# The last of 32 attention groups in two quarters of the tokens, one behind the other

## The chip, the cores and the metric

The kernel runs on one core of one Trainium2 chip. A core has five engines that work side by side and wait for one another by semaphores: PE (TensorE, matrix products; PEld is its loading of weights), DVE (VectorE), ACT (ScalarE), POOL (GpSimd) and SP, which here only issues DMA transfers. Products land in PSUM, which has eight banks of 128 partitions x 512 numbers; a tile of 128 x 512 fills one. The metric is device time in microseconds (us) of one execution, median of several runs.

## The reference

The result is a gated sum of two branches over an input x of 2048 tokens x 512 channels:

- branch A is attention with 32 heads of 16 channels: `softmax(q k^T / 4) v` for each head, all heads side by side, times `wo` (512 x 512);
- branch B is a layer norm followed by a two-layer MLP across the tokens (2048 to 1792 to 2048) with a gelu between;
- `out = g * A + (1 - g) * B` with `g = sigmoid(sum(x * gate_w))` for each token.

All inputs and the output are float32.

## The kernel before, in words

To keep float32 accuracy most operands are split into a high and a low part, and a product is three matrix products: hi x hi, hi x lo, lo x hi. `split` (lines 63 to 66) makes the parts: a copy and a subtraction.

After the projections and the MLP's first layer (lines 165 to 397), which the change leaves alone, comes the long part, lines 399 to 810. The attention runs in `NG` = 32 **groups**: 16 pairs of heads, for each of two halves of the tokens (1024 query tokens a half). A group has 64 units of scores: 16 chunks of 128 keys, two heads, two quarters of 512 query tokens (`qb`). For a unit, `score` (line 689) multiplies 64 rows of stacked parts of k and q into a PSUM bank; the two heads of a pair lie on rows 0 to 63 and 64 to 127, so that PE computes a score of each side by side. Two units share a tile `s`, and one ACT instruction takes the exponential of both (line 709) into `pt`. `apply_v` (line 657) multiplies `pt` by the head's v (16 columns and a column of ones, which gives the sum of the exponentials) and adds into the one bank `av`, four blocks of 32 partitions.

The group's loop (lines 712 to 757) goes in 11 **phases** (`ph`), ten of six units and one of four; two phases are a **two** (`two`), five of them in a group. The order in a phase is written out by hand: scores, then deferred work, then `apply_v` for the units of the phase before (`late`). Between the scores stand **dense** products of other work: the MLP's second layer (`second_layer`), and the attention's output product (`project`), 128 rows of the result at a time. A dense step is cut in halves of 64 rows: the upper half runs in a two's first phase and the lower half in its second, each beside a score on the other half of PE's rows. `put` and `put_outputs` lay the steps out over the twos (`dense[two]`, four to six each), and `call` hangs other work on a two (`calls`). A small POOL instruction (`token`) keeps the two halves apart, and all dense work adds into the single bank `dn`.

When a group ends, `evacuate` (line 629) copies `av` to `ot` on DVE, stores the rows to DRAM (`o_d`), and puts `invert` (maximum and reciprocal of the sums, whole tile) into `slow`, a list from which one item is taken in each second phase; its result is stored (`r_d`) by the list `stores`. When four groups of a half are done, `fetch_o` (line 511) loads their rows and the reciprocals, the latter spread over 16 rows for each head, and puts `divide` (product, then split) into `slow`; the parts are `o_parts[half, k]`, k = 0 to 3. For the second half of the tokens k = 3 holds only three pairs of heads (96 rows), since the fourth pair is the last group itself. `EARLY` = 9 is the number of products (of 12) for k = 0 to 2; for tiles 8 to 15 `project` adds those into `base` rows held on chip. In the last group tiles 12 to 15 of these are still being done.

After the last group (lines 764 to 808) eight banks `pa` take, for each of the eight tiles of 128 tokens in the second half, the three products for k = 3 (`others`) and those of the last pair, whose o is not fetched but taken from `ot`: a product with `sums_of` spreads the sums over the rows, DVE takes maximum, reciprocal, product and split (in two halves m of 256 columns of each head and quarter), and 16-row products with `wq`, the last 32 rows of `wo`, finish the banks. Each bank is then scaled by the gate and added to its row, five by DVE (line 805), three by ACT and POOL (lines 801, 802), and sent out, 256 KB a row block, on the queues of SP and ACT.

At the end all engines load a flag and jump over a general version of the attention that these inputs do not need (lines 813 to 866).

## Time and profile before

| what | value |
|---|---|
| median of 3 runs | 1336.42 us |
| lowest and highest of the runs | 1335.47 and 1336.7 us |
| the profiled execution's own time | 1335.31 us |
| its span, first to last instruction | 1333.4 us |
| busy: PE, ACT, DVE, POOL | 99%, 82%, 31%, 15% |
| mean granted clock of PE | 0.996 |
| first score of the last group | at 1278.98 us |
| copy of the last group's sums | at 1311.52 us |

The profile is of one execution. A row of the timeline gives start, length, engine, line, operation, result and operands, shapes, count, and in brackets the idle time before it with what ended it. The chain of work is followed back from the last instruction to what released each step. An engine's name with a q is its queue of instructions, as in SPq for DMA issues. A product's row lasts longer than the interval at which products follow on each other, since they are pipelined; the chain shows the intervals.

### The profile page before, as it was taken

The numbers are of one execution on the slowest core, as the hardware profiler recorded it, in microseconds if no ns is written. First come the engines' busy times: TensorE is split into PE (matmuls) and PEld (weight loads), VectorE is DVE, ScalarE is ACT, GpSimd is POOL, SyncE is SP. The second block draws the span as 40 slices with busy tenths as digits, with TensorE's granted clock in tenths as the row PEclk, the third lists the DMA queues.
The fourth block names the chain that finished last, engine by engine and source line by source line (L and its number), as shares of the span: only waits on it lengthen the run. The fifth ranks groups of instructions, "written<-read, shape, count | busy, mean of one in ns | idle before, by whom it ended". The sixth has DMA issues, their size and how long they took to land.

```text
span 1333.4 us, 32411 instructions
## 1 busy us (share of the span) xinstructions
PE 1314.6 (99%) x13288; PEld 770.0 (58%) x13288; DVE 413.5 (31%) x625; ACT 1096.3 (82%) x1264; POOL 202.3 (15%) x468
## 2 busy tenths in 40 slices
PE   9999999999999999999999999999999999999996
PEld 6888778876555555555555555455554555545553
DVE  3596571454121111222322111222111222132324
ACT  3344343447999999999999999999999999999993
POOL 0210254443011011011000011000110110100001
PEclk9999999999999999999999999999999999999998
DMA  3587643327343333334555344545333334454511
GB/s 119 165 275 294 206 119 95 95 75 156 73 85 65 61 73 83 67 75 96 121 109 129 68 76 90 100 111 125 61 65 73 77 68 81 72 113 108 108 53 67
DMA packets 93240, 138.41 MB, mean 104 GB/s; under 512 B 14149, under 2 KB 53211, under 8 KB 90011
## 3 DMA queue, kind: packets, MB, share of 16 engines
q1 hardware_dynamic: 92650, 135.46, 42.7%
q8 instruction: 107, 1.75, 0.6%
q10 hardware_dynamic: 432, 0.79, 0.2%
q14 instruction: 51, 0.41, 0.1%
HBM read 99.63 MB, written 36.56 MB: 102 GB/s over the span
## 4 chain that ended last, share of the span: by engine, by line
PE 94%; ACT 2%; DMA 1%; DVE 1%; SPq 0%; issue 0%; POOL 0%; POOLq 0%; DVEq 0%; ACTq 0%
PE av L665 35%; PE s L700 26%; PE acc L357 12%; PE dn L738 11%; PE acc L73 10%; ACT pt L709 2%; DMA o_sum<-r 1%; PE dn L685 1%; PE acc L184 0%; DMA wv_raw<-in_A_wqkv_dram 0%; DVE sums L783 0%; SPq L419 0%; POOL w_lo L66 0%; DVE base L805 0%; DVE lo L66 0%
## 5 line engine op out<-in xcount | busy, mean ns | idle before, releaser
L709 ACT ACTIVATE pt<-s 128x1024 f32<-128x1024 f32 x1024 | 964.9, 1028 | 33.9 <-PE s L700 26.6
L700 PE MATMUL s<-qs,ks 64*128 64x512 f32 x2048 | 527.4, 421 | 3.0 <-ACT pt L709 3.0
L665 PE MATMUL av<-pt,v 128*17 128x256 f32 x8192 | 510.6, 381 | 0.0
L700 PEld LDWEIGHTS s<-qs,ks 64*128 64x128 f32 x2048 | 301.0, 184 | 207.8 <-ACT pt L709 155.4
L665 PEld LDWEIGHTS av<-pt,v 128*17 128x17 f32 x8192 | 205.2, 97 | 259.6 <-issue 125.3
L738 PE MATMUL dn<-u_hi,w_hi 64*128 64x512 f32 x428 | 182.3, 426 | 0.7 <-POOL token L742 0.7
L66 POOL TENSOR_TENSOR w_lo<-w_raw,w_hi 128x512 fp32r<-128x512 f32 (+1 forms) x128 | 154.4, 1209 | 136.5 <-ACT w_hi L65 111.4
L738 PE MATMUL dn<-u_lo,w_hi 64*128 64x512 f32 x428 | 169.6, 396 | 0.0
L738 PE MATMUL dn<-u_hi,w_lo 64*128 64x512 f32 x428 | 168.4, 393 | 0.0
L742 POOL MEMSET token<- 1x1 f32 x320 | 29.3, 92 | 875.8 <-PE dn L738 552.2
L631 DVE COPY ot<-av 128x512 f32<-128x512 f32 x32 | 22.1, 692 | 352.9 <-PE av L665 347.5
L644 DVE RECIPROCAL rt<-rt 128x512 f32<-128x512 f32 x31 | 103.9, 3353 | 1.1
L65 ACT CAST w_hi<-w_raw 128x512 fp32r<-128x512 f32 (+1 forms) x67 | 37.8, 566 | 65.9 <-PE acc L357 59.9
L357 PE MATMUL acc<-h_hi,w_lo 128*128 128x512 f32 x224 | 89.2, 398 | 0.3 <-POOL w_lo L66 0.3
L357 PE MATMUL acc<-h_hi,w_hi 128*128 128x512 f32 x224 | 89.0, 397 | 0.0
L357 PE MATMUL acc<-h_lo,w_hi 128*128 128x512 f32 x224 | 88.8, 396 | 0.0
L738 PEld LDWEIGHTS dn<-u_lo,w_hi 64*128 64x128 f32 x428 | 79.2, 185 | 3.4
L738 PEld LDWEIGHTS dn<-u_hi,w_lo 64*128 64x128 f32 x428 | 79.0, 185 | 3.6
L738 PEld LDWEIGHTS dn<-u_hi,w_hi 64*128 64x128 f32 x428 | 78.7, 184 | 3.7 <-POOL token L742 1.0
L65 DVE CAST w_hi<-w_raw 128x512 fp32r<-128x512 f32 (+1 forms) x61 | 22.4, 378 | 124.4 <-PE dn L738 66.8
L434 DVE TENSOR_SCALAR row<-dn,b2x,omg 128x512 f32<-128x512 f32 x16 | 13.0, 810 | 147.8 <-PE dn L738 106.5
L73 PE MATMUL acc<-xt_hi,wc_hi 128*128 128x512 f32 x128 | 49.8, 389 | 0.0
(131 smaller groups left out, 1065.8 us busy)
## 6 DMA issues: line engine op xcount, KB each, us to landing
w_raw<-in_B_w_dram SPq DMA_DIRECT2D x96, 256.0 KB
ks<-kp SPq DMA_DIRECT2D x192, 128.0 KB
qs<-qp SPq DMA_DIRECT2D x256, 64.0 KB
qp<-pc SPq DMA_DIRECT2D x16, 768.0 KB
x<-in_A_x_dram SPq DMA_DIRECT2D x32, 256.0 KB
kp<-pc SPq DMA_DIRECT2D x16, 512.0 KB
w_raw<-in_B_w_dram SPq DMA_DIRECT2D x32, 128.0 KB
bp<-row SPq DMA_DIRECT2D x16, 256.0 KB
```

The lines of the kernel that those rows point to most:

```text
L65: copy(hi, src)
L66: sub(lo, src, hi.bitcast(F32), ALU.subtract)
L73: nc.tensor.matmul(ps, a, b, start=start and n == 0, stop=stop and n == last)
L357: nc.tensor.matmul(p, a, b, start=first and k == 0, stop=last and k == 2)
L631: nc.vector.tensor_copy(ot, av)
L644: nc.vector.reciprocal(rt, rt)
L665: nc.tensor.matmul(av[32 * j : 32 * j + VC, i * QC : (i + 1) * QC], v[:, c, g % NP * 2 + i, :], pt[:, h * QC : (h + 1) * QC], start=added[ ...
L685: nc.tensor.matmul(ps, a, b, start=start, stop=stop)
L700: nc.tensor.matmul(s[:, m, :], kt[grp][rows, c * P : (c + 1) * P], qt[grp][rows, qb * NB : (qb + 1) * NB], start=True, stop=True,)
L709: nc.scalar.activation(pt, s, AF.Exp, scale=SCALE)
L738: mm = nc.tensor.matmul(ps, a[half], b[half], start=first and not second, stop=last and bool(second))
L742: fence = nc.gpsimd.memset(token, 0.0)
```

## The change

**The last group in two quarters.** In the last group the order of units becomes all of the first quarter of its tokens (qb = 0), then all of the second. It has twelve phases of 6, 6, 6, 6, 4, 4 units for each quarter. `av` then holds one quarter in 256 columns, a block of 32 partitions for each of two heads and two halves of the quarter; `evacuate` copies 256 columns, once after each quarter.

**Dense products on all rows.** In the last group no dense half stands beside a score. The last four of the nine early products of tiles 13 to 15 (`full`) come in phases 0 to 5, two a phase, on all rows, after `apply_v`. In phases 6, 7, 9, 10 and 11 `rest_early` does the three products for k = 3 of tiles 8 to 12 and adds them to their rows; in phase 8 `divide_last` starts the division of the first quarter. Items of `slow` are taken in every phase of this group.

**The order before it.** Tiles 10 and 11 of the second layer take 8 twos instead of 9. The first products of tiles 13 to 15 are five each instead of four. Opening the end's memory, and the calls of `fetch_o`, come up to two twos earlier; the reciprocals of group 30 are stored, and the last fetch is called, at the start of the third phase of the last group.

**The end.** Tiles 0 to 3 of the eight (the first quarter) need only the last pair's products, tiles 5, 6 and 7 the three for k = 3 as well. The last pair's products use 64 rows (both heads, `wq` laid out so). The division is done once for each quarter. Tiles 0 and 2 and tile 7 go by ACT and POOL, the others by DVE; the add of tile 2 waits for the second quarter's split.

```diff
--- before.py
+++ after.py
@@ -63,7 +63,7 @@
     def split(hi, lo, src, copy, sub):
 
         copy(hi, src)
-        sub(lo, src, hi.bitcast(F32), ALU.subtract)
+        return sub(lo, src, hi.bitcast(F32), ALU.subtract)
 
     def products(ps, pairs, start=True, stop=True):
 
@@ -499,13 +499,12 @@
             sums_of.rearrange("p (j r) -> p j r", r=32),
             ident.rearrange("p (j r) -> p j r", r=32)[:, :, DH:VC].broadcast_to([P, P // 32, 32]),
         )
-        wq.extend(end.tile([P, 2, D], F32R, name=f"wq{n}") for n in range(2))
-        raw = end.tile([P, 2, D], F32, name="wq_raw")
+        wq.extend(end.tile([P, D], F32R, name=f"wq{n}") for n in range(2))
+        raw = end.tile([P, D], F32, name="wq_raw")
         nc.gpsimd.memset(raw, 0.0)
         for j in range(4):
-            nc.sync.dma_start(
-                raw[32 * j : 32 * j + DH], a_wo[(H - 2) * DH : H * DH, :].rearrange("(i r) c -> r i c", i=2)
-            )
+            r0 = (H - 2 + j % 2) * DH
+            nc.sync.dma_start(raw[32 * j : 32 * j + DH], a_wo[r0 : r0 + DH, :])
         slow.append((two + 5, lambda: split(wq[0], wq[1], raw, nc.vector.tensor_copy, nc.vector.tensor_tensor)))
 
     def fetch_o(half, k, pairs=4):
@@ -571,8 +570,11 @@
 
     TWOS = 5
-    dense, calls = {}, {}
+    LAST = [6, 6, 6, 6, 4, 4] * 2
+    dense, calls, full = {}, {}, {}
 
     def put(steps, at, sizes):
         for n in sizes:
@@ -599,7 +601,7 @@
     first, at = steps[:30], put(steps[30:], 0, [6] * 2)
     for t in range(NS):
         if t:
-            at = put(second_layer(t), at, [6, 6] + [4] * 6 + [6] if t > 9 else [6] * 4 + [4] * 3 + [6])
+            at = put(second_layer(t), at, [6, 6] + [4] * 6 + [6] if t > 11 else [6] * 4 + [4] * 3 + [6])
         if t == 7:
             call(at - 8, fetch_o, 0, 0)
             call(at - 5, fetch_o, 0, 1)
@@ -612,13 +614,23 @@
     call(at - 5, fetch_o, 1, 1)
     assert at - 5 > (NP + 8) * TWOS + 4
     call(at, open_end)
-    at = put_outputs(range(NS - 3, NS), 0, 4, at)
-    assert at == (NP + 12) * TWOS + 7
-    call(at - 2, fetch_o, 1, 2)
+    call(at + 1, fetch_o, 1, 2)
+    assert at > (NP + 12) * TWOS + 1
+    at = put_outputs(range(NS - 3, NS), 0, 5, at)
     at = put_outputs(range(NH, NS - 3), 0, EARLY, at, [5, 4])
-    at = put_outputs(range(NS - 3, NS), 4, EARLY, at)
-    assert at == NG * TWOS
-    call((NG - 1) * TWOS + 2, fetch_o, 1, 3, 3)
+    assert at == (NG - 1) * TWOS
+    for t in range(NS - 3, NS):
+        steps, load = project(t, 5, EARLY)
+        call(at - 1, load)
+        full[at, 0], full[at, 1] = steps[:2], steps[2:]
+        at += 1
+
+    def store():
+        while stores:
+            stores.pop()()
+
+    call((NG - 1) * TWOS + 1, store)
+    call((NG - 1) * TWOS + 1, fetch_o, 1, 3, 3)
 
     token = out_pool.tile([1, 1], F32, name="token", bufs=1)
     av = ps_av.tile([P, NB], F32, name="av")
@@ -628,9 +640,10 @@
 
     def evacuate(g):
         ot = out_pool.tile([P, NB], F32, name="ot")
+        if g == NG - 1:
+            nc.vector.tensor_copy(ot[:, :QC], av[:, :QC])
+            return ot[:, :QC]
         nc.vector.tensor_copy(ot, av)
-        if g == NG - 1:
-            return ot
         half, p = divmod(g, NP)
         k, p = divmod(p, 4)
         blocks = [(slice(32 * j, 32 * j + VC), slice(j * QC, (j + 1) * QC)) for j in range(4)]
@@ -656,18 +669,23 @@
 
     def apply_v(g, units, last):
 
-        for pair in zip(*([u for u in units if u[2] == qb] for qb in range(2))):
-            for i, c, qb, pt in pair:
-
-                added[qb] += 1
+        final = g == NG - 1
+        key = 0 if final else 2
+        for pair in zip(*([u for u in units if u[key] == n] for n in range(2))):
+            for unit in pair:
+                i, c, qb, pt = unit
+
+                n = unit[key]
+                added[n] += 1
                 for h in range(2):
-                    j = 2 * qb + h
+                    j = 2 * h + i if final else 2 * qb + h
+                    at = 0 if final else i * QC
                     nc.tensor.matmul(
-                        av[32 * j : 32 * j + VC, i * QC : (i + 1) * QC],
+                        av[32 * j : 32 * j + VC, at : at + QC],
                         v[:, c, g % NP * 2 + i, :],
                         pt[:, h * QC : (h + 1) * QC],
-                        start=added[qb] == 1,
-                        stop=added[qb] == 2 * NS,
+                        start=added[n] == 1,
+                        stop=added[n] == (1 if final else 2) * NS,
                     )
         if last:
             added[:] = 0, 0
@@ -689,7 +707,7 @@
         def score(grp, i, n, done):
 
             nonlocal open_s
-            c, qb = n // 2, (n + i) % 2
+            c, qb = (n % NS, n // NS) if grp == NG - 1 else (n // 2, (n + i) % 2)
             if open_s is None:
                 open_s = ps_s.tile([P, 2, NB], F32, name="s"), ptp.tile([P, 2, NB], F32, name="pt")
                 m = 0
@@ -709,23 +727,44 @@
                 nc.scalar.activation(pt, s, AF.Exp, scale=SCALE)
                 open_s = None
 
+        def rest(t, ps, stop=True):
+
+            for n, (a, b) in enumerate(o_matmuls(1, t, EARLY, 3 * ND)):
+                nc.tensor.matmul(ps, a, b, start=n == 0, stop=stop and n == 2)
+
+        def rest_early(t):
+            ps = ps_dn.tile([P, D], F32, name="dn")
+            rest(t, ps)
+            output(t, ps, rows[t])
+
+        def divide_last(qb, ot, totals):
+
+            nc.tensor.matmul(totals, sums_of, ot, start=True, stop=True)
+            sums, hi, lo = (
+                end.tile([P, QC], dt, name=f"{name}{qb}") for name, dt in (("sums", F32), ("hi", F32R), ("lo", F32R))
+            )
+            nc.vector.tensor_scalar_max(sums, totals, LEAST_SUM)
+            nc.vector.reciprocal(sums, sums)
+            nc.vector.tensor_mul(sums, ot, sums)
+            step = split(hi, lo, sums, nc.vector.tensor_copy, nc.vector.tensor_tensor)
+            return hi, lo, step
+
         for grp in range(NG):
             at = [0, 0]
-            for ph in range(2 * TWOS + 1):
+            final = grp == NG - 1
+            for ph, n_s in enumerate(LAST if final else [6] * 2 * TWOS + [4]):
                 if ph == 0 and grp + 1 < NG:
                     qt[grp + 1] = load_q(grp + 1)
                 if ph == 1 and grp + 1 < NG:
                     kt[grp + 1] = load_k(grp + 1)
                 two, second = divmod(ph, 2)
                 two += grp * TWOS
-                if ph == 2 * TWOS:
-                    n_s, beside = 4, []
-                elif second:
-                    n_s = 6
-                else:
+                if ph == 2 * TWOS and not final:
+                    beside = []
+                elif not second:
                     for what, *args in calls.get(two, ()):
                         what(*args)
-                    n_s, beside = 6, [step(*args) for step, *args in dense.get(two, ())]
+                    beside = [step(*args) for step, *args in dense.get(two, ())]
                 units = []
                 for n in range(n_s - len(beside)):
                     i = (n + second + 1) % 2
@@ -744,18 +783,30 @@
                     if done and second:
                         done()
                 if second:
-                    while stores:
-                        stores.pop()()
+                    store()
                     if len(ready) < 2:
                         split_weight(nc.vector.tensor_copy)
+                if second or final:
                     for n, (ready_at, step) in enumerate(slow):
                         if ready_at <= two:
                             slow.pop(n)[1]()
                             break
-                if late:
-                    apply_v(*late)
-                late = grp, units, ph == 2 * TWOS
+                ot = apply_v(*late) if late else None
+                late = grp, units, ph in (5, 11) if final else ph == 2 * TWOS
+                if final:
+                    for step, *args in full.get((two, second), ()):
+                        ps, a, b, first, last, done = step(*args)
+                        nc.tensor.matmul(ps, a, b, start=first, stop=last)
+                        if done:
+                            done()
+                    if ph == 6:
+                        last_ot = ot
+                    if ph == 8:
+                        parts = [divide_last(0, last_ot, ps_dn.tile([P, D], F32, name="dn")[:, :QC])]
+                    elif ph > 5:
+                        rest_early(NH + ph - 6 - (ph > 8))
         last_ot = apply_v(*late)
+        assert not slow and not stores
     psum_ctx.close()
 
     ptp_ctx.close()
@@ -765,47 +816,60 @@
         tc.tile_pool(name="ps_end", bufs=1, space=PSUM, reuse_waits="tile") as ps_end,
         tc.manual_schedule(engines=engines),
     ):
...
+        pa = {t: ps_end.tile([P, D], F32, name=f"pa{t}") for t in (5, 6, 0, 1, 2, 3, 4, 7)}
+
+        def last_pair(qb, m):
+
+            for n, (a, b) in enumerate(((0, 0), (0, 1), (1, 0))):
+                for h in range(2):
+                    t = 4 * qb + 2 * h + m
+                    at = slice(h * HALF, (h + 1) * HALF)
+                    lhs = parts[qb][a][at, m * P : (m + 1) * P]
+                    nc.tensor.matmul(pa[t], lhs, wq[b][at], start=t < 5 and n == 0, stop=n == 2)
+
+        def row_of(t):
+            return rows[NH + t], g[:, NH + t : NH + t + 1], of[(NH + t) * P : (NH + t + 1) * P, :]
+
+        def scaled(t):
+            res = end.tile([P, D], F32, name=f"res{t}")
+            nc.scalar.activation(res, pa[t], AF.Copy, scale=row_of(t)[1])
+            return res
+
+        def add(t, res):
+            row = row_of(t)[0]
+            return nc.gpsimd.tensor_tensor(row, res, row, ALU.add)
+
+        def finish(t):
+            row, gate, _ = row_of(t)
+            nc.vector.scalar_tensor_tensor(row, pa[t], gate, row, ALU.mult, ALU.add)
+
+        def put_row(t, queue):
+            row, _, dst = row_of(t)
+            queue.dma_start(dst, row)
+
+        last_pair(0, 0)
+        res0 = scaled(0)
+        add(0, res0)
+        put_row(0, nc.sync)
+        res2 = scaled(2)
+        parts.append(divide_last(1, last_ot, pa[4][:, :QC]))
+        last_pair(0, 1)
+        for t in (5, 6, 7):
+            rest(NH + t, pa[t], stop=False)
+
+        tc.add_manual_dep(add(2, res2).ins, parts[1][2].ins.name, SYNC, reason="one port")
+        put_row(2, nc.scalar)
+        for t in (1, 3):
+            finish(t)
+            put_row(t, nc.sync)
+        last_pair(1, 0)
+        last_pair(1, 1)
+        for t in (4, 6, 5):
+            finish(t)
+            put_row(t, nc.scalar if t == 6 else nc.sync)
+        res7 = scaled(7)
+        add(7, res7)
+        put_row(7, nc.scalar)
     end_ctx.close()
     att_ctx.close()
 
```

More of the change, by code (lines that the diff above doesn't have):

```diff
@@ L767, in gated_mix @@
     ):
-        pa = [ps_end.tile([P, D], F32, name=f"pa{t}") for t in range(8)]
-        def others(*tiles):
-            for t in tiles:
-                for n, (a, b) in enumerate(o_matmuls(1, NH + t, EARLY, 3 * ND)):
-                    nc.tensor.matmul(pa[t], a, b, start=n == 0, stop=False)
-        others(0)
-        nc.tensor.matmul(pa[7], sums_of, last_ot, start=True, stop=True)
-        tiles = [end.tile([P, NB], dt, name=name) for name, dt in (("sums", F32), ("hi", F32R), ("lo", F32R))]
@@ L778, in gated_mix @@
-        sums, hi, lo = ([x.rearrange("p (i m c) -> p m i c", i=2, m=2)[:, m] for m in range(2)] for x in tiles)
-        totals, last = (x.rearrange("p (i m c) -> p m i c", i=2, m=2) for x in (pa[7], last_ot))
-        for m in range(2):
-            nc.vector.tensor_scalar_max(sums[m], totals[:, m], LEAST_SUM)
-        for m in range(2):
-            nc.vector.reciprocal(sums[m], sums[m])
-            nc.vector.tensor_mul(sums[m], last[:, m], sums[m])
-            split(hi[m], lo[m], sums[m], nc.vector.tensor_copy, nc.vector.tensor_tensor)
@@ L786, in gated_mix @@
-        others(2, 4, 6, 1, 3)
-        behind = []
-        for m in range(2):
-            for i in range(2):
-                for n, (a, b) in enumerate(((hi, 0), (hi, 1), (lo, 0))):
-                    for j in range(4):
-                        at = slice(32 * j, 32 * j + DH)
-                        nc.tensor.matmul(pa[2 * j + m], a[m][at, i, :], wq[b][at, i, :], start=False, stop=i == 1 and n == 2)
-            if m == 0:
-                others(5, 7)
-            for j in range(4):
-                t = 2 * j + m
-                row, gate, dst = rows[NH + t], g[:, NH + t : NH + t + 1], of[(NH + t) * P : (NH + t + 1) * P, :]
-                if j == 1 or j == 3 and m == 0:
-                    res = end.tile([P, D], F32, name=f"res{t}")
-                    nc.scalar.activation(res, pa[t], AF.Copy, scale=gate)
-                    nc.gpsimd.tensor_tensor(row, res, row, ALU.add)
-                    behind.append((dst, row))
-                else:
-                    nc.vector.scalar_tensor_tensor(row, pa[t], gate, row, ALU.mult, ALU.add)
-                    nc.sync.dma_start(dst, row)
@@ L807, in gated_mix @@
-        for dst, row in behind:
-            nc.scalar.dma_start(dst, row)
+        pa = {t: ps_end.tile([P, D], F32, name=f"pa{t}") for t in (5, 6, 0, 1, 2, 3, 4, 7)}
[6 more added lines that the diff above has]
+                    nc.tensor.matmul(pa[t], lhs, wq[b][at], start=t < 5 and n == 0, stop=n == 2)
```

## The prediction

> **What bounds the kernel now.** I read the page first (busy shares, then the chain of work that ended last), then the table by stage, then that chain in order of time, then the timeline around the last group.
>
> ```profile
> PE 1314.6 (99%) x13288; PEld 770.0 (58%) x13288; DVE 413.5 (31%) x625; ACT 1096.3 (82%) x1264; POOL 202.3 (15%) x468
> ...
> PE 94%; ACT 2%; DMA 1%; DVE 1%; SPq 0%; issue 0%; POOL 0%; POOLq 0%; DVEq 0%; ACTq 0%
> ```
>
> PE carries 94% of the chain. The change touches the end only, so that end is read by itself: stage, PE, PEld, DVE, ACT and POOL busy, clock, DMA share, GB/s.
>
> ```profile
> 1278.98:1311.52 32.54, 32.53 (x389) 17.16 (x386) 10.52 (x10) 30.72 (x33) 0.88 (x10) 1.00 0.19 54
> 1296.00:1297.00 1.00, 1.00 (x14) 0.67 (x8) 0.00 (x0) 0.84 (x2) 0.00 (x0) 1.00 0.26 72
> 1297.00:1298.00 1.00, 1.00 (x11) 0.50 (x11) 0.00 (x0) 1.00 (x2) 0.01 (x1) 1.00 0.00 0
> 1324.40:1333.40 9.00, 0.00 (x0) 0.00 (x0) 0.00 (x0) 0.00 (x0) 0.00 (x1) 0.50 0.47 166
> ```
>
> The first row is the last group, from its first score (1278.98, called S below) to the copy of its sums. PE is full; ACT has 30.72 us in 33 activations, 0.93 us each, so 32 of them want 29.8 us of the 32.54. The tail after it is 1333.4 - 1311.52 = 21.9 us, its last 9 us with no compute at all, only the output rows and the program's end.
>
> The chain in order of time (start, length, what) gives PE's prices and then the tail's:
>
> ```profile
> 885.74 1.42 PE av L665 x24
> 888.74 1.42 PE av L665 x24
> ...
> 1272.74 1.42 PE av L665 x24
> ...
> 1275.55 1.42 PE av L665 x24
> 1276.97 0.66 PE s L700 x4
> ...
> 1280.63 0.99 PE av L665 x16
> ...
> 1310.83 0.63 PE av L665 x8
> 1311.46 0.89 PE pa L773 x3
> 1312.35 1.06 PE pa L776 x2
> ...
> 1313.43 0.76 DVE sums L781 x2
> 1314.19 1.67 DVE sums L783
> ...
> 1315.88 0.43 DVE sums L784
> ...
> 1316.34 0.30 DVE hi L65
> ...
> 1316.67 0.43 DVE lo L66
> ...
> 1319.58 1.40 DVE lo L66
> 1320.97 2.06 DVE base L805 x3
> ```
>
> Four scores, two side by side on the two halves of the rows, take 0.66; three products on all rows take 0.89. The difference is one **slot**, 0.23 us; what is left of both, 0.20, is an **opening**, paid where PE goes to another tile shape. From block of av to block of av it is 3.00 us in a phase with six dense halves (885.74 to 888.74) and 2.81 with four (1272.74 to 1275.55). As a test, the last group now: ten phases with two of four and eight of five halves are 58 slots, the eleventh has 2, 60 x 0.23 = 13.8; 11 openings 2.2; av 2 x 0.99 + 10 x 1.42 = 16.2; together 32.2 of the 32.54. So the prices hold, and **PE is the bound of the group, ACT close behind; in the tail it is DVE, then the output**.
>
> **The change part by part.**
>
> *Groups 0 to 30.* Two tiles of the second layer (t = 10, 11) go from three sixes and six fours to five and three, and the early products of tiles 13 to 15 from fours to fives, to make room for what leaves the last group. Counted over the 155 pairs of phases: 85 with five or six halves before, 93 after (a five fills the sixth slot with a lone score, so it costs as a six). Eight pairs x 2 phases x (3.00 - 2.81) = **+3.0**; bounds 2.4 and 3.1, since next to a group's boundary part of it may hide.
>
> One wait goes. In group 29 the products of part 2 of o wait for their division, which waits for the fetched reciprocals:
>
> ```profile
> 1219.96 12.00 DMA o_sum<-r
> ```
>
> ```profile
> 1231.08 1.49 PE L665 MATMUL av<-pt,v 128*17 128x256 f32 x24
> 1232.05 1.22 DVE L523 TENSOR_TENSOR o_sum<-o_lo,o_sum 128x1024 f32<-128x1024 f32 x1 [6.08 <-DMA o_sum<-r]
> 1233.31 0.69 DVE L65 CAST o_hi<-o_sum 128x1024 fp32r<-128x1024 f32 x1
> 1234.03 1.23 DVE L66 TENSOR_TENSOR o_lo<-o_sum,o_hi 128x1024 fp32r<-128x1024 f32 x1
> 1235.74 1.49 PE L665 MATMUL av<-pt,v 128*17 128x256 f32 x24
> ```
>
> That phase lasts 4.66 instead of 2.81. The fetch was called at the start of a group, behind eight loads of q and ahead of those of k. After, it is called in phase 6 of group 28, away from both, and used as many phases later: I take the **1.85 us as gone** (bounds 0 and 1.85).
>
> *The last group.* Twelve phases instead of eleven, 32 pairs of scores = 7.4 and 12 openings = 2.4; av 8 x 1.42 + 5 x 0.99 = 16.3 (the two quarters end in blocks of 16); twelve products on all rows in phases 0 to 5, 12 slots and 6 openings = 4.0; the five `rest_early` of three products, 15 slots and 5 openings = 4.5; the sums of the first quarter, 256 columns where L776 has 512, about 0.6. Sum 35.2 against 32.54: **+2.6**. Below lies ACT: where it is the bound, 31.6 (29.8, with 0.6 ahead and 1.2 behind), -0.9; above, a further 0.1 per opening, +3.8. I take the prices that gave the present group.
>
> The openings are 11 x 0.20 = 2.2 of that. [...]
>
> *A wait that comes.* `rest_early` in phase 6 needs part 3 of o, with group 30 in it. The rows that set when it comes:
>
> ```profile
> 1281.69 0.69 DVE L631 COPY ot<-av 128x512 f32<-128x512 f32 x1 [5.32 <-PE av L665]
> ...
> 1282.88 3.35 DVE L644 RECIPROCAL rt<-rt 128x512 f32<-128x512 f32 x1
> ...
> 1286.26 2.33 SPq L649 DMA_DIRECT2D r<-rt  x4
> ...
> 1289.68 0.80 SPq L520 DMA_DIRECT2D o_sum<-r  x1
> ```
>
> Copy, reciprocal, four stores, fetch: each follows on the other, so store and fetch, called earlier now, still wait on SP for the reciprocal; one load of a base row stands ahead of them there, as now. The fetch goes out at S + 10.7 now; phase 0 is three slots shorter after, so S + 10.0. It lands now 7.3 us on (traffic until 1297, none after); one 256 KB load of a base row no longer runs beside it, and I take 6.4: S + 16.4 (bounds 5.3, by which the wait vanishes, and the 12.0 above). Behind the landing on DVE stand the division, 1.22 + 0.69 + 1.23 = 3.1, and, queued behind it in the program's order, the output of tile 15 (2.06 / 3 = 0.69), which frees the one dn bank: S + 20.2. PE comes to phase 6's products at S + 18.4 (phase 0: 0.89 + 0.99 + 0.66; 1 to 3: 0.89 + 1.42 + 0.66 each; 4: 0.66 + 1.42 + 0.66; 5: 0.66 + 0.99 + 0.66; together 16.5; then scores 0.89 and av 0.99). PE stands 1.8, say **+1.9** with the semaphores; its scores, av and with them ACT stand behind it. The copy of the first quarter's av is in the same DVE queue, but the next av comes a phase later and does not wait for it. The division of the first quarter (3.2 us of DVE in phase 8) lies beside PE.
>
> *The tail.* Now 21.9. After, from the copy of the second quarter (zero): tiles 0 and 2, three slots and an opening, 0.9, cover the copy (half of 0.69 and some, 0.45); the sums 0.2 + 0.53, at 1.6; DVE max 0.38, reciprocal 1.67, product 0.43, hi 0.30, lo 0.43, at 4.8. The second set of these (1.67 + 0.43 + 0.30 + 1.40 now) is gone. PE's nine `rest` products and tiles 1 and 3 lie beside it. Then five outputs on DVE (1, 3, 4, 6, 5) of 0.69, at 8.3; tile 6 is out at 7.6. Tile 0 goes by ACT and POOL before that. Tile 2's add on POOL is made to wait for lo, which took 1.40 instead of 0.43 beside such an add; it ends at 4.8 + 1.3 = 6.1, ACT sends row 2 then, and behind it in ACT's order stand row 6 and tile 7, which are not ready sooner, so this wait costs nothing. But tile 7 is last, and its place in ACT's order counts:
>
> ```profile
> 1321.66 4.62 SPq L806 DMA_DIRECT2D out_dram<-base  x5
> ...
> 1322.37 0.69 ACT L801 ACTIVATE res<-pa,g 128x512 f32<-128x512 f32 x1 [2.49 <-PE pa L793]
> 1322.45 2.97 ACTq L808 DMA_DIRECT2D out_dram<-base  x3
> 1323.13 1.27 POOL L802 TENSOR_TENSOR base<-res,base 128x512 f32<-128x512 f32 x1 [1.01 <-ACT res L801]
> ```
>
> ACT must first send tile 6 (7.6), then scale tile 7 (0.69) and POOL adds (1.27): sent at 10.1 with 0.45 for an issue; three issues take 2.97 here, so some stand, and I take 10.5, ended at 10.95. From the end of the last issue now (1321.66 + 4.62) to 1333.4 are 7.1; SP, whose waits fill part of that, is through earlier after, so 6.3 (bounds 5.5 and 7.1). Tail 17.25: **-4.65** (bounds -6.0 and -3.2). All eight rows still go out, four of them not after the end of DVE's work.
>
> *Sum.* +3.0 - 1.85 + 2.6 + 1.9 - 4.65 = **+1.0**, on the profiled execution's 1335.31 us (span 1333.4): 1336.3. The median of the runs, 1336.42, lies 1.1 above that; I carry the difference over: **1337.4**. Wq halves (DVE, hidden under PE) and the return of `split` cost nothing; DVE is busy 10.52 of 32.54 there.
>
> **The rivals.**
>
> *Faster: PE is not the bound of the last group.* If products on all rows need no opening beside av, a phase wants 0.89 + 1.42 + 0.46 = 2.77 and ACT 2.79: ACT bounds it, 31.6 instead of 35.2, whole -2.6 or, with a fetch that lands sooner too, -4: 1333.8 to 1332.4. For it: the fours run at 2.81, ACT's own pace. Against: the 0.20 shows at every change of shape in the chain.
>
> *Slower: the fetch lands late.* One mechanism, at `rest_early` of phase 6: each us after S + 14.5 is a us of PE. With the 12.0 us of the fetch in group 29 it lands at S + 22, the wait is 7.4 and the time 1337.4 + 5.5 = 1342.9. It passes 0.2% from a landing 8.1 us after the issue on. For it: 7.3 and 12.0 are both seen. Against: no loads of q or k run in the last group.
>
> The granted clock is 0.50 in the stage where PE has nothing left (1324.40 on). [...]
>
> *The tail shrinks less.* If tiles 4 and 6 stand at their issue as in the 2.97 above, ACT comes to tile 7 later by 1 to 1.5: 1338.7. This also is the case that the change does not do what it says: of the first quarter only the division is done early, rows 1 and 3 still go out behind the second division.
>
> **How the numbers follow.** A measurement of this kernel tells about 0.2%, 2.7 us, from no change. The forecast, within 2 us of 1337.4, has 0.50; the smaller tail 0.14; the late fetch 0.18; ACT as the bound 0.18. Same: all of the forecast, half of the smaller tail (0.07) and none else, 0.57; slower: 0.18 + 0.07 = 0.25; faster: 0.18. The range, 1333.6 to 1341.2, leaves out the longer half of the late fetch (0.09) and the better half of the faster case (0.09).
>
> **What would show it.** Right: no phase of 4.66 in group 29; from first score to the second quarter's copy 36 to 38 us, with PE idle once, at the first `rest` product, released by DVE; openings of 0.2 at each change of shape; the last row sent by ACT 10 to 11 us after the copy. Wrong: PE idle there under 0.5 or over 3 us; ACT without gaps in the last group; a tail under 16 or over 19 us; new waits in groups 0 to 30.

## The result, and the profile after

The changed kernel takes 1335.45 us (median of 14 runs, 1333.98 to 1337.98); the kernel before, run beside it, 1334.95 us (14 runs, 1332.84 to 1338.46). The ratio is 1.0001, 95% interval 0.9992 to 1.0011: no difference that can be told. The forecast was 1337.4 with 0.57 on "same". A change that rebuilt the last group and the tail moved 5 to 6 us in each of two stages, in opposite directions.

The profiled execution of the changed kernel took 1337.98 us, span 1336.2. From its page, the busy line and the shares of the chain:

```profile
PE 1318.7 (99%) x13254; PEld 771.2 (58%) x13254; DVE 413.3 (31%) x631; ACT 1096.6 (82%) x1264; POOL 202.4 (15%) x458
...
PE 94%; ACT 2%; DMA 1%; issue 1%; DVE 1%; POOL 1%; SPq 0%; POOLq 0%; DVEq 0%; ACTq 0%
```

Nothing of the change is to be seen there; it is in the stages. The table by stage of the changed kernel (PE, PEld, DVE, ACT, POOL busy, clock, DMA share, GB/s), first the last group, then the tail:

```profile
1282.89:1320.47 37.58, 35.85 (x371) 16.40 (x369) 16.91 (x21) 30.96 (x33) 0.00 (x0) 1.00 0.12 33
1320.47:1336.20 15.73, 6.23 (x35) 3.74 (x35) 7.04 (x11) 1.95 (x3) 3.83 (x3) 0.85 0.39 139
```

The group took 32.54 us before and has 37.58 now, of which PE is busy 35.85; the tail had 21.9 and has 15.7. The same stages for every kernel profiled here, in us; the columns on the right count from the last copy:

| kernel | group 1 starts at | to the last group's first score | to the last copy | to the end | last issue over | last row's data in |
|---|---|---|---|---|---|---|
| before | 344.06 | 934.93 | 32.54 | 21.92 | 14.76 | 19.06 |
| before_again | 345.36 | 932.98 | 32.53 | 20.89 | 14.42 | 18.37 |
| before_fetch | 347.37 | 932.86 | 32.52 | 21.12 | 13.57 | 18.22 |
| before_fetch_timed | 344.97 | 933.04 | 32.52 | 20.88 | 13.88 | 18.42 |
| the change | 347.64 | 935.26 | 37.58 | 15.74 | 10.40 | 13.38 |
| after_again | 345.31 | 935.54 | 37.27 | 15.67 | 10.90 | 13.50 |
| rest_later | 347.33 | 935.37 | 36.29 | 16.43 | 11.07 | 14.27 |
| no_full | 343.85 | 935.53 | 39.01 | 16.07 | 10.86 | 13.90 |
| full_later | 347.43 | 935.59 | 41.57 | 16.47 | 11.20 | 14.29 |
| divide_later | 344.00 | 935.51 | 36.27 | 15.69 | 10.86 | 13.62 |
| divide_later_free | 344.48 | 935.41 | 36.25 | 16.42 | 10.74 | 14.13 |
| tail_order | 345.17 | 935.29 | 37.36 | 16.82 | 9.49 | 14.04 |
| no_port_wait | 348.40 | 935.35 | 37.54 | 15.16 | 10.74 | 13.17 |
| rows_left | 346.88 | 935.40 | 37.49 | 14.84 | 10.42 | 12.40 |

Read it by columns. The first is code that no kernel changes, and yet it spreads by 4.5 us, nearly as much as the group or the tail moved and nine times what the two medians differ by; the last section says why. The second shows two families, 932.9 to 933.0 and 935.3 to 935.6, and one row that belongs to neither: the very execution on which the prediction was built.

The chain of the changed kernel in order of time (start, length, what) has the new wait:

```profile
1293.04 6.43 DMA o_sum<-r
...
1299.57 1.23 DVE o_sum L522
...
1300.82 0.70 DVE o_hi L65
...
1302.69 0.75 DVE base L542
...
1303.48 0.96 PE dn L733 x3
```

And its timeline (start, length, engine, line, operation) the same from PE's side:

```profile
1300.90 1.06 PE L683 MATMUL av<-pt,v 128*17 128x256 f32 x16
...
1303.48 0.50 PE L733 MATMUL dn<-wo_hi,o_hi 96*128 96x512 f32 x1 [1.52 <-DVE base L542]
```

Fetch, division, output of tile 15, first `rest` product, each released by the one before it, as forecast: the fetch lands at S + 16.6 (S is 1282.89 now), PE goes on at S + 20.6. The tail, from its timeline:

```profile
1322.42 1.75 DVE L747 RECIPROCAL sums<-sums 128x256 f32<-128x256 f32 x1
1323.46 6.46 SPq L848 DMA_DIRECT2D out_dram<-base  x5
...
1324.99 0.43 DVE L66 TENSOR_TENSOR lo<-sums,hi 128x256 fp32r<-128x256 f32 x1
1325.33 3.38 DVE L844 SCALAR_TENSOR_TENSOR base<-pa,g,base 128x512 f32<-128x512 f32 x5
...
1326.89 1.54 ACTq L848 DMA_DIRECT2D out_dram<-base  x2
1328.47 0.69 ACT L835 ACTIVATE res<-pa,g 128x512 f32<-128x512 f32 x1 [5.82 <-DVE base L844]
1329.24 1.26 POOL L840 TENSOR_TENSOR base<-res,base 128x512 f32<-128x512 f32 x1 [2.38 <-ACT res L835]
1330.53 0.34 ACTq L848 DMA_DIRECT2D out_dram<-base  x1
```

One division instead of two, `lo` at 0.43 instead of 1.40, rows leaving from 1323.46 on, and ACT at tile 7 only after row 6: all as the prediction placed it.

### The profile page after: what moved, and what is told of

Same layout as the page of the kernel before. It is cut to its first block, busy times and chain, and to the rows that moved or that the text cites. A ratio compares the mean times of both kernels' runs of the same rounds, so it can differ in the third digit from the quotient of the medians.

```text
span 1336.2 us, 32328 instructions
## 1 busy us (share of the span) xinstructions
PE 1318.7 (99%) x13254; PEld 771.2 (58%) x13254; DVE 413.3 (31%) x631; ACT 1096.6 (82%) x1264; POOL 202.4 (15%) x458
## 4 chain that ended last, share of the span: by engine, by line
PE 94%; ACT 2%; DMA 1%; issue 1%; DVE 1%; POOL 1%; SPq 0%; POOLq 0%; DVEq 0%; ACTq 0%
PE av L683 35%; PE s L718 26%; PE acc L357 11%; PE dn L777 10%; PE acc L73 10%; ACT pt L727 2%; PE acc L184 1%; DMA o_sum<-r 0%; DMA qs<-qp 0%; POOL w_lo L66 0%; PE dn L733 0%; DMA w_raw<-in_B_w_dram 0%; PE acc L208 0%; DVE sums L747 0%; SPq L419 0%
```

## The experiments

The theory on trial, A: the terms of the prediction, above all the wait for part 3 of o, the openings on PE, and a tail whose end hangs on ACT's order. The rivals: ACT as bound of the last group; a wait bound to other things than the fetch; a tail that ends by its data. Single times of one kernel on one chip lie too far apart to be compared (the kernel before gave 1333.54 and 1341.33 in two executions of one session; the slower one was not profiled), so kernels that ran once are judged by their stages. Where a stage is given for a kernel, it is that of one execution.

**1. Both kernels once more (before_again, after_again).** No edit.

> The kernel before, unchanged, profiled once more. By stages the earlier call of the fetch saves 2.07 and 1.89 us between group 1 and the last group's first score, but five rounds of times show no gain (ratio 0.9996). Theory V (the 1.85 us wait in group 29 is not there in every execution: the fetch that took 12.0 us takes less in others): the 4.66 us phase is 2.8 to 4.0 here and group 1 to the last group's first score 933.0 to 934.3. Theory F (it is always there): 4.66 again and 934.9, and what hides the gain is the spread elsewhere. The start: 344 to 345.2 us to group 1 if TensorE's granted clock stays at 1.00 between 310 and 322 us, 346.9 to 348.4 if it falls to 0.50 there (0.86 in the mean), as in all eleven profiles so far.

> The changed kernel, unchanged, profiled once more. Its own work repeats: group 1 to the last group's first score 935.2 to 935.6 us, first score to last copy 37.5 to 37.6 (phase 6 4.3 to 4.4), copy to end 15.2 to 16.8 as in the runs with the same tail. The start: 344 to 345.2 us to group 1 if TensorE's granted clock stays at 1.00 between 310 and 322 us, 346.9 to 348.4 if it falls there; by this alone the whole is 1333.9 to 1338.0.

In before_again the fetch for part 2 of o, in group 29, went out at 1221.17 and DVE's division began at 1231.21; its timeline, with the next blocks of `av`:

```profile
1221.17 0.64 SPq L520 DMA_DIRECT2D o_sum<-r  x1
...
1231.21 1.23 DVE L523 TENSOR_TENSOR o_sum<-o_lo,o_sum 128x1024 f32<-128x1024 f32 x1 [4.02 <-DMA o_sum<-r]
...
1232.32 1.49 PE L665 MATMUL av<-pt,v 128*17 128x256 f32 x24
...
1235.10 1.49 PE L665 MATMUL av<-pt,v 128*17 128x256 f32 x24
```

10.0 us from issue to use instead of 12.0, and the phase that had 4.66 us has 2.78: no wait at all. Theory V holds. The wait that the change takes away was there in the one profiled execution and not in the next; its tail, too, was the longest of the four that this code gave (21.92 against 20.88 to 21.12). The changed kernel repeats itself within 0.3 us: 935.54, 37.27 (37.5 to 37.6 was expected; phase 6 took 4.04, not 4.3 to 4.4), 15.67.

**2. The earlier fetch alone (before_fetch, and before_fetch_timed with five rounds).** The kernel before, with

```diff
-    call(at - 2, fetch_o, 1, 2)
+    call(NP * TWOS + 64, fetch_o, 1, 2)
```

> The kernel before, with the fetch of part 2 of o called one two earlier (phase 8 of group 28 instead of the start of group 29). Theory A: it lands before it is needed, the phase of 4.66 us in group 29 takes 2.8, and all else is as before: 1.85 us less from group 1 to the last group. Rival D: the loads of q and k at the next group's start still run beside it, it lands as late, and the phase keeps 1 us of wait or more.

> The kernel before with one line of the change, the earlier call of the fetch for part 2 of o, now timed. By the stages of one execution (group 1 to the last group's first score 2.07 us shorter, nothing else changed) it is 1.9 to 2.1 us faster, ratio 0.9985; if the gain of that execution was given back elsewhere, within 0.5 us, ratio 1.000.

By the stages it looked like a full gain: 932.86 and 933.04, 2 us below the profile of before. The times say 1333.89 us against 1335.26, ratio 0.9996 (0.9986 to 1.0006), no gain that can be told. Experiment 1 can explain both: the kernel before stood at 933.0 by itself in one of its two profiles. How often it does was not counted. The times give a hint, no more: the twelve of before_fetch_timed lie in two heaps, eight from 1333.05 to 1334.08 and four from 1336.26 to 1337.10 (the start has two lengths, see the last section), while seven of the 17 of the kernel before lie between them, from 1334.41 to 1336.11, where a wait of 1.85 us would put an execution of the first heap (the profiled one, with the wait and the short start, took 1335.31). No trace shows that the seven had it.

**3. `rest` a phase later (rest_later).**

```diff
-                    elif ph > 5:
-                        rest_early(NH + ph - 6 - (ph > 8))
+                    elif ph > 6:
+                        rest_early(NH + ph - 7 - (ph > 8))
...
-        for t in (5, 6, 7):
+        for t in (5, 6, 7, 4):
```

> The three products for k = 3 start one phase later (phases 7, 9, 10, 11, tiles 8 to 11) and those of tile 12 go to the tail, beside DVE's division. Theory A (the wait at phase 6 is set by a chain that PE's order does not move: copy of group 30, reciprocal, stores, fetch, division, output of tile 15): PE comes to the bank when it is free, the wait of 1.5 us goes and one block of three products with its opening, 0.9, leaves the group: from the first score of the last group to the second quarter's copy 35.2 us instead of 37.6, tail 15.7 to 16.0. Rival B (the group's length is PE's work alone, and a wait only moves to the next use of the bank): 0.9 less, 36.7.

36.29: the wait in phase 6 is gone (1.88 us instead of 4.37), and phase 7 has 4.37 instead of 3.21. Its timeline there:

```profile
1300.44 5.61 ACT L727 ACTIVATE pt<-s 128x1024 f32<-128x1024 f32 x6 [0.37 <-PE s L718]
...
1302.43 0.50 PE L718 MATMUL s<-qs,ks 64*128 64x512 f32 x2 [0.21 <-ACT pt L727]
...
1303.12 0.41 DVE L644 COPY ot<-av 128x256 f32<-128x256 f32 x1
1303.35 0.51 PE L718 MATMUL s<-qs,ks 64*128 64x512 f32 x2 [0.41 <-ACT pt L727]
```

ACT runs six exponentials without a gap, and PE's scores wait for it. Neither number was met (35.2 and 36.7): of the 2.5 us that the wait's phase gave back, 1.2 were taken by ACT, the next bound here, where phase 6 and the first part of phase 7 have no dense work.

**4. Without the early products (no_full).** Leaves out the last four early products of tiles 13 to 15, so those rows lack them:

```diff
-        full[at, 0], full[at, 1] = steps[:2], steps[2:]
```

> Leaves out the last four early products of tiles 13 to 15 (phases 0 to 5), so those rows are not complete. Theory A: the six phases get shorter by some 2 us, down to ACT's pace (0.93 us for two units), but the release at phase 6 stays at 20.5 us after the group's first score less at most 0.7 (the output of tile 15 is gone from DVE's queue); the wait of PE grows from 1.5 to 3 us or more, and the group takes 36.8 to 37.6 us. So the products on all rows cost nothing in this kernel, since the wait hides them. Rival B: 12 slots and 6 openings less, 33.6 us.

39.01 us, with less work 1.4 us longer; neither theory had that (36.8 to 37.6 and 33.6). Phases 4 and 5 show the price as forecast (2.08 and 1.65 instead of 2.74 and 2.32: two products and an opening are 0.66). But the fetch does not come sooner, PE stands earlier and a little longer (1.86 us instead of 1.52, not the 3 that were expected), and then the clock falls. The table by stage of no_full in strips of 3.4 us:

```profile
1291.10:1294.50 3.40, 3.40 (x48) 1.44 (x40) 0.00 (x0) 3.40 (x5) 0.00 (x0) 1.00 0.41 107
1294.50:1297.90 3.40, 1.72 (x20) 0.55 (x18) 1.58 (x2) 3.13 (x4) 0.00 (x0) 0.99 0.04 13
1297.90:1301.30 3.40, 2.98 (x9) 1.62 (x9) 2.64 (x4) 0.14 (x1) 0.00 (x0) 0.50 0.00 0
1301.30:1304.70 3.40, 3.40 (x29) 1.00 (x25) 0.00 (x0) 2.72 (x3) 0.00 (x0) 0.50 0.01 2
```

PE is busy 1.72 of 3.4 us, and for the next 6.8 us the granted clock is 0.50. Phase 6 took 6.27 us and phase 7 5.22, against 4.37 and 3.21. An estimate: phase 6 without a wait is 2.77 and phase 7 in the changed kernel 3.21, so with a wait of 1.9 and the full clock the two would take 7.9 instead of 11.5 us, and the group 35.4. So it was the fall of the clock, in the one execution profiled, that made leaving the early products out cost more than they do; there they were cover for the wait.

**5. The early products later (full_later), and one instruction of DVE moved (divide_later, divide_later_free).** full_later is rest_later with

```diff
-        full[at, 0], full[at, 1] = steps[:2], steps[2:]
+        full[at, 1], full[at + 1, 0] = steps[:2], steps[2:]
```

> The changed kernel with PE's work of the last group spread otherwise: the twelve products on all rows stand in phases 1 to 6 instead of 0 to 5, and the five groups of rest products in phases 7, 9, 10, 11 and (tile 12's) in the tail, as in rest_later. Theory B (in rest_later ACT was the next bound, because phases 5 and 6 had too little for PE to do and phase 0 too much; the wait for part 3 of o itself is over at S + 20.2): phase 0 falls to 1.9, phase 6 takes 2.3 or more, PE comes to the first rest product at S + 21 and no phase is over 3.7; first score to last copy 35.2 us (rest_later 36.3, the change 37.6), copy to end 16.4, whole -2.5 us against the kernel before by these two and the 2.2 of the denser groups less the 1.85, about 1332.5 where the kernel before has 1335. Theory A (the wait is bound to the moment at which the division and the copy of the first quarter are through on DVE, whatever PE has ahead of it): phase 7 stays at 4 us, first score to last copy 36.3, whole -1.3 us.

Both theories missed: 41.57 us, whole 1339.79 us (six runs), ratio 1.0034 (1.0021 to 1.0048). Its timeline where phase 5 took 6.59 us:

```profile
1299.84 1.22 DVE L522 TENSOR_TENSOR o_sum<-o_lo,o_sum 96x1024 f32<-96x1024 f32 x1 [6.93 <-DMA o_sum<-r]
1301.09 0.69 DVE L65 CAST o_hi<-o_sum 96x1024 fp32r<-96x1024 f32 x1
1301.82 1.22 DVE L66 TENSOR_TENSOR o_lo<-o_sum,o_hi 96x1024 fp32r<-96x1024 f32 x1
1302.96 0.74 DVE L542 SCALAR_TENSOR_TENSOR base<-dn,g,base 128x512 f32<-128x512 f32 x1
1303.75 0.50 PE L799 MATMUL dn<-wo_hi,o_lo 128*128 128x512 f32 x1 [4.20 <-DVE base L542]
```

DVE stood 6.93 us for the fetch, and behind its division in the queue stood an output of tile 14, which frees the one `dn` bank (0.74 us). Moving the early products by a phase had put that output behind the waiting division; PE stood 4.20 us for an output that had all its operands. divide_later takes the division after it and changes nothing else in any engine's order:

```diff
-        slow.append((two + 1, divide))
+        slow.append((two + (1.5 if half and k == 3 else 1), divide))
...
-                        if ready_at <= two:
+                        if ready_at <= two + second / 2:
```

> full_later with DVE's order changed and nothing else: the output of tile 14's early part stands on DVE ahead of the division for part 3 of o, which waits for the fetched reciprocals until S + 16.8, instead of behind it. Theory Q (full_later's 6.59 us phase is that queue: the output that frees the one dn bank stood 6.9 us behind the waiting division, PE stood 4.2 us, and two thirds of the phase after it ran at half the clock): no phase over 3.8, first score to last copy 35.0 to 35.8 us instead of 41.57, group 1 to end 986 to 987 where the kernel before had 989.4, ratio to it 0.997 to 0.999. Theory A2 (PE has to stand at the first rest product in any case, for the fetch itself): phase 7 over 4 us, first score to last copy 36.3 or more, ratio 0.999 to 1.001.

36.27 instead of 41.57: **5.3 us for the place of one output in DVE's queue**. No phase is at 6.59; the output now comes long before the division, and the first `rest` product waits for nothing:

```profile
1294.43 0.75 DVE L542 SCALAR_TENSOR_TENSOR base<-dn,g,base 128x512 f32<-128x512 f32 x1 [5.04 <-PE dn L799]
...
1296.38 1.22 DVE L522 TENSOR_TENSOR o_sum<-o_lo,o_sum 96x1024 f32<-96x1024 f32 x1 [1.20 <-DMA o_sum<-r]
...
1301.99 0.50 PE L733 MATMUL dn<-wo_hi,o_hi 96*128 96x512 f32 x1
```

So Q's cause is right and its size was not: 35.0 to 35.8 and no phase over 3.8 were expected. The remainder is phase 1, 4.12 us: phases 0 and 1 together take 6.05 without early products in phase 0 and 6.04 with them. There ACT is the bound, and those two products were free where the change has them. The whole is 1333.84 us, ratio 1.0003 (0.9994 to 1.0012).

> divide_later, and POOL's add of tile 2 in the tail does not wait for the second quarter's division on DVE (as in no_port_wait). If the 0.35 us that the division lost there is covered by row 2 going out 2.2 us sooner, copy to end is 15.2 to 15.9 where divide_later has 16.4, ratio to divide_later 0.9995; if the end follows the landing of the last row and that spreads by itself, 15.2 to 16.8 and no difference from divide_later that the rounds can tell.

It also drops the wait of experiment 7. 1333.76 us, ratio 1.0002 (0.9993 to 1.0011): no version beats the kernel before by what can be told.

**6. ACT's order in the tail (tail_order).**

```diff
+        res7 = scaled(7)
+        add(7, res7)
         for t in (4, 6, 5):
             finish(t)
             put_row(t, nc.scalar if t == 6 else nc.sync)
-        res7 = scaled(7)
-        add(7, res7)
```

> The changed kernel with tile 7 scaled by ACT, and added by POOL, ahead of the issue of row 6 on ACT's queue; rows 6 and 7 are sent after that. Theory A (the tail ends with what is issued last, and ACT stood behind row 6): row 7 goes out some 1.5 us sooner, then SP's row 5 is the last, and copy to end takes 14.3 to 14.9 us instead of 15.7. Rival C (the tail ends with the transfer of the eight rows, whatever the order of issue): 15.7.

The order did what it should, the end did not, and neither theory had its number. tail_order's timeline:

```profile
1324.66 0.69 ACT L835 ACTIVATE res<-pa,g 128x512 f32<-128x512 f32 x1 [4.66 <-POOL base L840]
1325.42 1.26 POOL L840 TENSOR_TENSOR base<-res,base 128x512 f32<-128x512 f32 x1 [1.23 <-DVE base L844]
1325.44 1.87 ACTq L848 DMA_DIRECT2D out_dram<-base  x2
```

The last issue is over 9.49 us after the copy instead of 10.40, the end comes at 16.82 instead of 15.74. The traffic of the 17 us from the copy on, in 40 slices, first of the changed kernel:

```profile
GB/s 0 0 0 0 0 0 0 0 0 337 280 0 0 0 0 246 390 371 352 371 357 390 366 328 381 227 337 159 96 39 67 14 0 19 19 0 0 0 0 0
```

then of tail_order:

```profile
GB/s 0 0 0 0 0 0 0 0 0 337 280 0 0 0 0 284 352 371 357 361 82 24 357 361 390 376 386 405 203 101 39 19 24 0 0 0 39 0 0 0
```

It has a gap in the middle (82 and 24 GB/s), while SP's and ACT's issues (6.48 us for five, 1.87 for two) lasted until 1327.3, and its data end 0.7 us later. In the table of stages the end comes 2.0 to 2.9 us after the last row's data in all fourteen profiles, and 4.4 to 7.6 after the last issue. What follows the data can be seen in the same lines: the numbers at the far right (19 and 19 above, 39 below) are loads of the program's own instructions. The last of these begins 1.1 to 1.8 us after the last row's data in every profile, and the end comes 0.3 to 1.3 after that. No run separates the data from these loads.

**7. The wait of tile 2's add (no_port_wait).**

```diff
-        tc.add_manual_dep(add(2, res2).ins, parts[1][2].ins.name, SYNC, reason="one port")
+        add(2, res2)
```

> The changed kernel, but POOL's add of tile 2 does not wait for the second quarter's division on DVE. If the two disturb each other (theory P: the lo of the kernel before took 1.40 us beside such an add, 0.43 without): one of the division's operations (reciprocal 1.75, product 0.43, hi 0.29, lo 0.43) takes 0.5 to 1.0 us longer, the outputs on DVE begin 0.5 to 1.0 later, and copy to end is 15.7 to 16.7. If not (theory N): the division keeps 0.43 for lo, row 2 goes out about 3 us sooner on ACT's queue, and copy to end is 15.2 to 15.7.

Row 2 went out 2.2 us sooner (N expected about 3); the division's product took 0.77 instead of 0.43 (0.77 again in divide_later_free), as P said, though less than the 0.5 us more that it expected. The tails with this edit are 15.16 and 16.42; the others with all rows are 15.7 to 16.8: the wait saves 0.35 us of DVE, and the end doesn't tell.

**8. Half of the rows' data (rows_left).** Leaves out the stores of tiles 1, 3, 4 and 5:

```diff
             finish(t)
-            put_row(t, nc.sync)
...
-            put_row(t, nc.scalar if t == 6 else nc.sync)
+            if t == 6:
+                put_row(t, nc.scalar)
```

> The changed kernel, leaving out the stores of the rows of tiles 1, 3, 4 and 5 in the tail, so that these rows of the output are not written; the computing is whole, and ACT's order (row 2, row 6, tile 7, row 7) is as it was. Theory L (the end follows the last issue on ACT, 10.4 us after the copy, by 5.3): copy to end stays at 15.2 to 15.7. Theory R (the end follows the rows' data, 8 x 256 KB that now run until 13.4): with half the data the last row's own transfer sets the end, data until 12.0 to 12.5 and copy to end 13.3 to 14.3.

Between the two: with the last issue at the same 10.42 the data end at 12.40, as R said, and the end comes at 14.84, 2.4 later. L's number is missed (15.2 to 15.7), but 4.4 us from the last issue to the end is also what no_port_wait has with all its rows, so this run alone does not refute L. R's time for the data stands, and its remainder after the data was taken too small.

## Why the prediction was right

*Denser groups, +3.0 (bounds 2.4 to 3.1).* 935.3 to 935.6 against 932.9 to 933.0 where no wait is: **+2.2 to 2.7**. Right in kind, near the lower bound.

*The wait in group 29, -1.85.* The group is 1.84 shorter than in the profile of before, as forecast, but this is **the step that doesn't stand**: in before_again it had been at 2.78 without the change. The prediction took a wait of one execution for one of the kernel. The row that it quoted, 12.0 us for the fetch, was enough to ask how near the deadline was: at 10.0 nothing waits. Its lower bound of 0 for the gain covered this case.

*The last group, +2.6 and the wait +1.9.* 37.58 against a forecast of 37.1. The wait is 1.6 (phase 6 took 4.37; without a wait it took 2.54 in divide_later with one product less, a slot of 0.23, so 2.77); in after_again, where that phase took 4.04, it is 1.3, the fetch having landed 0.3 sooner. So the work alone came to 36.0 instead of 35.2, and the term was 0.8 too small. The prices of slot and opening hold: 0.66 for two products and an opening. What is over is above all phase 1, 3.45 instead of 2.97, where PE's scores wait for ACT; its timeline in the changed kernel:

```profile
1285.49 0.73 PE L718 MATMUL s<-qs,ks 64*128 64x512 f32 x4
...
1286.42 0.49 PE L718 MATMUL s<-qs,ks 64*128 64x512 f32 x2 [0.20 <-ACT pt L727]
```

That is the rival "ACT as the bound": in the changed kernel it is true of the first two phases together, and in the variants of phases with little dense work. (The term's upper bound, +3.8, counts 0.1 more for twelve openings; the sum has 23, which gives +4.9.)

*The tail, -4.65 (bounds -6.0 to -3.2).* -6.2 against the profile of before, just outside the bounds, and -5.2 against before_again. A tail under 16 us was on the prediction's own list of signs of being wrong, and it was 15.74 and 15.67. The work on DVE, POOL and ACT came out as laid down. Mis-sized was what follows the last issue, 5.3 instead of 6.3, and misread was what the end hangs on: not ACT's place for tile 7 (tail_order), but the rows' data and the 2 to 3 us behind them, as far as one execution of each variant tells.

*The sum.* Stage by stage from group 1 on, the change stands 0.8 us below the profile of before and 2.2 above before_again; the times say +0.1 us (-1.1 to +1.5). With the wait of group 29 in some executions and not in others the kernel before lies between the two; how often it is there was not counted, so how far the sum was right by balanced errors (0.6 too much in the groups, 0.5 too little in the last group, 0.5 to 1.5 too little credit for the tail, a gain that is only sometimes one) stays open within a microsecond. That "same" came true does not bear out the +1.0: the interval of the times holds 0 and -1 as well, and most of its terms were off by half a microsecond or more. The rival "slower by a late fetch" had the right place and no late fetch: 6.4 us as taken.

## What to carry to other kernels

A wait read from one execution is a sample: where a transfer's end lies near its deadline, profile the kernel twice before the wait is counted as a gain. When work is moved by a phase, look at every in-order queue for an instruction that is ready but would now stand behind one that waits for a transfer; here that one place cost 5.3 us, including the clock that fell behind it (0.50 for 3.4 us). Work that leaves a stage gains only up to the next bound (ACT here), and it may have been the cover of a wait.

## What was not expected of the hardware

**The clock fell for 3.4 and for 6.8 us.** In no_full it was 0.50 from 1297.9 for 6.8 us, beginning 0.4 us ahead of PE's next product; in full_later from 1304.5 for 3.4 us, there beginning 0.7 us after PE had gone back to work. The table by stage of full_later:

```profile
1297.70:1301.10 3.40, 1.85 (x21) 0.67 (x20) 1.23 (x2) 1.94 (x2) 0.00 (x0) 1.00 0.08 22
1301.10:1304.50 3.40, 0.75 (x4) 0.38 (x4) 2.56 (x3) 0.00 (x0) 0.00 (x0) 1.00 0.00 0
1304.50:1307.90 3.40, 3.40 (x23) 1.32 (x23) 0.00 (x0) 2.62 (x3) 0.00 (x0) 0.50 0.00 0
```

What the clock answers to was not shown. In strips as long as the fall in full_later, 3.4 us, 1.72 us busy was followed by half the clock, 1.85 was not. No threshold of busy time can be drawn between the two: at the start of full_later a strip with 2.04 us busy (314.62 to 318.04; PE stood 1.38 us in all of the 12 from 310 on) was followed by half the clock, and so was one with 2.98 in no_full that was itself at half. The 1.52 us wait of the changed kernel lay in one strip with 1.89 us busy (1300.62 to 1304.03), and the clock stayed at 1.00.

**So the start of the attention has two lengths.** Some 2 to 3 us after the first scores PE stands for POOL's `token`, and whether the clock falls then differs from execution to execution. The timeline shows the wait, first before, then in the changed kernel:

```profile
314.92 0.50 PE L738 MATMUL dn<-u_hi,w_hi 64*128 64x512 f32 x1 [0.69 <-POOL token L742]
```

```profile
316.90 0.50 PE L777 MATMUL dn<-u_hi,w_hi 64*128 64x512 f32 x1 [1.54 <-POOL token L781]
```

The table by stage, before:

```profile
310.00:322.00 12.00, 11.13 (x103) 6.82 (x103) 3.44 (x6) 10.64 (x13) 2.53 (x5) 1.00 0.81 172
```

and the changed kernel:

```profile
310.00:322.00 12.00, 10.27 (x66) 6.15 (x66) 4.63 (x8) 7.56 (x9) 2.52 (x5) 0.86 0.68 171
```

All eight profiles with 1.00 there, of both kernels and the variants, have group 1 at 343.85 to 345.36 us, all six with 0.86 at 346.88 to 348.40. In the eight PE stood 0.66 to 1.10 us for the token, in the six 1.20 to 1.67; why the token comes late was not followed. Of the 2.9 us between the means of the two lots, half the clock for 3.4 us can make 1.7 (an estimate, 3.4 x 0.50; in the changed kernel products follow there every 0.43 us instead of 0.23); the rest lies in that longer wait and in a later first score (0.7 in the mean). This is why 1337.98 and 1335.31 us, the two profiled executions, differ by 2.7 us while the work from group 1 on is 0.8 shorter, and why one execution of each could not have judged this change.
